# Moving twenty row-scaling products from ScalarE and VectorE to GpSimd, in front of the scatters that read them

## The chip, the cores and the metric

The kernel runs on one core of a Trainium2 chip. The metric is device time of one execution in microseconds (us), the median of several runs. Engines are named as in the profile: PE is TensorE's matmul (PEld its weight load), DVE is VectorE, ACT is ScalarE, POOL is GpSimd, SP is SyncE, which here only issues transfers. Every engine works through its own queue in order, and waits at an instruction whose input is not there yet.

## The reference

Three layers follow each other. The first is a delta-rule attention over 4 batches, 8 heads, 768 positions and head size 48: a 48x48 state per head is read by the query and then updated with each key and value. The second routes each of the 3072 rows of 384 numbers to one of 8 experts. The third is a dense layer with an ELU.

```python
logits = xn @ en.T / tau
expert_idx = np.argmax(logits, axis=1)
probs = np.exp(logits - logits.max(-1, keepdims=True))
probs /= probs.sum(-1, keepdims=True) + 1e-09
gate_w = probs[np.arange(N), expert_idx]
for e in range(E):
    mask = expert_idx == e
    h = np.maximum(x[mask] @ w1[e], 0.0)
    out[mask] = gate_w[mask, None] * (h @ w2[e])
```

The gate weight is positive, so the kernel multiplies each row by it before the expert: `gate * (relu(x w1) w2)` is `relu((gate * x) w1) w2`.

## The kernel before, in words

Attention is done in 12 chunks of 64 positions. A chunk has a chain of solve steps on PE (`chain`, in two halves of the heads), each step evacuated by ACT or DVE; it needs the chunk's prepared keys (`lane`), its queries and values (`rest`), the state that the chunk before left, and the inverse of small triangular blocks. `invert(g)` makes that inverse for the two chunks 2g and 2g+1 at once: on POOL, 30 short tensor-tensor steps that each need the one before (line 1369), then two transposes on DVE (line 1374, `a<-T`), then four transfers into `bdT` (line 1378). The first solve of chunk 2g is the PE group `pw<-rh,bdT` that reads it. Beside these steps POOL prepares keys, queries and values (lines 1107, 1338, 1326), copies blocks for PE (`bd`, line 1220, tiles `bdS`, `bdZ`), and zeroes the next inverse's buffer (lines 1358 and 1360).

A chunk's output leaves PE as rows: `to_rows` puts them into one of four slots of the tile `xt` (line 1529 on ACT or DVE, "xput"). `route` then runs after chunks 1, 3, 5, 7 and 9 on all four slots, and after chunks 10 and 11 on two slots each. It finds each row's expert and place, and its gate weight `gs` (lines 341 and 342 on DVE). Then, for each slot, it multiplies the 384 columns of 128 rows by the gate weight, in place (the "gate" product), and scatters the rows to a buffer in device memory: a one-element memset on POOL (line 347) and an indirect transfer issued by POOL (line 348). After the four scatters POOL adds 128 to the row numbers in `xt` (line 359). A slot can be filled by the next xput only when the scatter that reads it has landed. The routings are numbered 1 to 7 here, in order of time; 1 to 5 have four gate products each.

The gate product has two ways, ACT (line 354) and DVE (line 355). Which way each of the 24 takes stands in the string `WAYS["gate"]`, one digit per product. The order of all work in this stage is fixed by hand: `STARTS` has one number per operation (hundredths of a planned us), and `replay` emits the operations in the order of these numbers. An operation that changes its engine keeps its number, and so its place in that order. The five routings' first gate products have the numbers 14342, 18682, 23603, 27537 and 31581. In the second and the fourth routing two inversion steps follow behind that number and ahead of the first scatter (18688 and 18740, 27546 and 27598), in the first and the third routing one (14389, 23646), in the fifth none. The scatters keep their order: in routing 1, for instance, slots 2, 3, 1, 0.

After attention the experts and the dense layer follow, bound by PE; their first step needs the table of rows that the last routing makes.

Of the kernel before, what the change touches and what calls it, by code (L numbers as in the profile page):

```python
# [12 lines left out]
ALU = mybir.AluOpType  # L13
AX = mybir.AxisListType

NT, DM, NE, F1, F2 = 3072, 384, 8, 1024, 2048
# [190 lines left out]
class Moe(Ops):  # L207
# [92 lines left out]
    def route(self, a, xt, first, step, last):  # L300

        nc, dv, part = self.nc, self.nc.vector, slice(first, None, step)
# [5 lines left out]
        lg, ex, oh, ss, sr, rn, mx, gs, di = (x[:, part] for x in (self.lg, self.ex, self.oh, self.ss, self.sr, self.rn, self.mx, self.gs, self.di))  # L308
# [29 lines left out]
        for b in tiles:  # L338
            a.act(NE + 140, lambda b=b: nc.scalar.activation(out=self.lgp[:, b, 0], in_=self.lg[:, b], func=AF.Exp, scale=self.rn[:, b:b + 1], accum_out=self.gs[:, b:b + 1]),
                  r=["rn", "lg", f"lgp{b}"], w=[f"gs{b}"])  # L340
# [5 lines left out]
        def scatter(b):  # L346
            nc.gpsimd.memset(self.gap, 0.0)
            i = nc.gpsimd.indirect_dma_start(
                out=self.xs, out_offset=bass.IndirectOffsetOnAxis(ap=self.di[:, b:b + 1], axis=0), in_=xt[:, b], in_offset=None)
            apart(self.tc, i, sent)  # L350

        for b in tiles:
            x, g = xt[:, b, :DM], self.gs[:, b:b + 1]
            a.op("gate", ("ACT", DM + 155, lambda x=x, g=g: nc.scalar.activation(out=x, in_=x, func=AF.Copy, scale=g)),
                    ("DVE", DM - 130, lambda x=x, g=g: dv.tensor_scalar(out=x, in0=x, scalar1=g, scalar2=None, op0=ALU.mult)), r=["gs"], w=[f"xt{b}"])
            a.pl.add("POOL", 1.04, lambda b=b: scatter(b), r=[f"xt{b}", "di", f"xid{b}", "xz", *xs], move=0.55)
        if not last:
            xi = xt.bitcast(I32)[:, part, DM]
# [671 lines left out]
class Attn(Ops):  # L1030
# [510 lines left out]
    "clear": "1111201310302011123201",  # L1541
    "dg": "010100100110000111110001001000001010001000100000",
    "evac": "000010001100001010000000000000000001010100000111010000001001000000101000100101000001100000001100000011110001000000010000000001000000011101001010010110000010110001011110011110100000000000001000",
    "gate": "000010010111011011011000",
    "gramA": "675664710346200673657401",
    "gramL": "310001010002161015667366",
    "invert": "111111",
# [208 lines left out]
```

## Time and profile before

| | us |
|---|---|
| median of 3 runs | 953.64 |
| the runs | 951.24, 953.64, 955.93 |
| the profiled execution | 954.83 |
| its span in the profile | 953.4 |

The profiled execution is 1.2 us above the median. A row of the time line of an engine has the start, the duration, the engine, the line of the kernel, the operation, the tiles that it writes and reads, the shape and the count; in brackets at its end stands how long the engine was idle before it and what ended that. Times are us from the start of the span. Attention and routing fill the first 357 us of it.

### The profile page before, as it was taken

The page shows a single profiled execution, that of the slowest core. Times are in us where ns is not written, and L with a number is a line of the kernel's source. Part 1 is how long each engine was busy: PE and PEld are TensorE (multiplying, and loading weights), DVE is VectorE, ACT ScalarE, POOL GpSimd, SP SyncE. Part 2 cuts the span into 40 slices and gives each one's busy share as a digit, 9 for nine tenths or more (in the row PEclk, how much of TensorE's full clock was granted, in tenths as well). Part 3 has the DMA queues.
Part 4 walks back from the last instruction along what each step waited for, and adds up shares of the span by engine and source line. Part 5 has one row for each costly group of instructions (what it writes and reads, how often), then busy time and mean ns, then how long its engine had stood idle before and what let it go on. Part 6 is the DMA issues. An engine that isn't in the chain of part 4 may idle for free.

```text
span 953.4 us, 28791 instructions
## 1 busy us (share of the span) xinstructions
PE 834.9 (88%) x11734; PEld 695.9 (73%) x11735; DVE 768.4 (81%) x1563; ACT 600.4 (63%) x1094; POOL 464.6 (49%) x707
## 2 busy tenths in 40 slices
PE   0537888798999877999999999889999999999995
PEld 0426788687888764555556568789999999999995
DVE  6787878778787963988898988998887887787884
ACT  8896779877786954455646636666545455465652
POOL 6564677676776432143433412354345555355452
PEclk9958999999999997999999999999999999999998
DMA  6667865847545418867899263210010100100000
GB/s 207 163 133 204 235 151 114 177 110 136 131 106 140 148 51 267 174 226 196 238 251 212 92 119 98 84 51 18 1 51 18 51 19 18 35 18 18 18 18 18
DMA packets 115365, 107.58 MB, mean 113 GB/s; under 512 B 72889, under 2 KB 100317, under 8 KB 114973
## 3 DMA queue, kind: packets, MB, share of 16 engines
q1 hardware_dynamic: 108649, 82.98, 35.8%
q0 software_dynamic: 6080, 22.05, 7.5%
q8 instruction: 93, 1.52, 0.7%
q10 hardware_dynamic: 500, 0.68, 0.3%
q14 instruction: 43, 0.35, 0.1%
HBM read 74.72 MB, written 19.97 MB: 99 GB/s over the span
## 4 chain that ended last, share of the span: by engine, by line
PE 49%; DVE 7%; issue 2%; DMA 2%; ACT 1%; SPq 0%; POOL 0%; POOLq 0%; DVEq 0%; ACTq 0%
PE pa L662 17%; PE acc L682 15%; PE acc L620 8%; PE pa L601 8%; DMA st<-in_w 2%; DVE w L519 1%; DVE wbl L676 1%; DVE w L518 1%; DVE dal L534 1%; DVE hl L615 0%; DVE wal L668 0%; SPq L471 0%; DVE dbl L534 0%; DVE wah L669 0%; PE pa L573 0%
## 5 line engine op out<-in xcount | busy, mean ns | idle before, releaser
L682 PE MATMUL acc<-dbh,wbl 128*128 128x192 f16 x672 | 165.3, 246 | 1.4 <-DVE wbl L676 1.4
L682 PE MATMUL acc<-dbl,wbh 128*128 128x192 f16 x672 | 165.3, 246 | 0.9 <-DVE dbl L534 0.9
L682 PE MATMUL acc<-dbh,wbh 128*128 128x192 f16 x672 | 165.3, 246 | 0.2 <-DVE y L630 0.2
L662 PE MATMUL pa<-x,dah 128*128 128x256 f16 x1152 | 157.3, 273 | 1.8 <-DVE wal L668 1.4
L682 PEld LDWEIGHTS <-wbh 128*128 128x128 f16 x1344 | 121.9, 98 | 1.5 <-issue 0.3
L662 PEld LDWEIGHTS <-dah 128*128 128x128 f16 x1152 | 111.9, 98 | 14.7 <-issue 2.0
L662 PE MATMUL pa<-x,dal 128*128 128x256 f16 x576 | 94.4, 273 | 0.9 <-DVE dal L534 0.9
L601 PE MATMUL pa<-x,wah 128*128 128x440 f16 (+6 forms) x384 | 77.0, 337 | 1.9 <-DVE hl L615 1.8
L1223 PEld LDWEIGHTS <-bdKT 112*128 112x128 f16 x1680 | 58.3, 101 | 21.0 <-ACT bdKT L1219 6.1
L1223 PEld LDWEIGHTS <-bdK 128*128 128x128 f16 x960 | 40.8, 119 | 42.8 <-ACT rh L1100 18.5
L669 POOL TENSOR_TENSOR wal<-wal 128x256 f32<-128x256 f32 (+1 forms) x67 | 44.8, 669 | 54.9 <-DVE wal L668 31.1
L675 ACT CAST wbh<-wal 128x384 f16<-128x384 f32 (+1 forms) x73 | 41.3, 566 | 44.8 <-PE acc L682 20.4
L682 PEld LDWEIGHTS <-wbl 128*128 128x128 f16 x672 | 65.7, 98 | 3.1 <-DVE wbl L676 2.1
L620 PE MATMUL acc<-hh,wbh 128*128 128x440 f16 (+6 forms) x192 | 64.2, 334 | 2.0 <-DVE y L630 1.1
L620 PE MATMUL acc<-hl,wbh 128*128 128x440 f16 (+6 forms) x192 | 64.1, 334 | 1.2 <-DVE hl L615 1.1
L614 ACT ACTIVATE hh<-pa 128x440 f16<-128x440 f32 (+6 forms) x64 | 31.9, 504 | 52.2 <-PE acc L620 24.8
L620 PE MATMUL acc<-hh,wbl 128*128 128x440 f16 (+6 forms) x192 | 64.0, 334 | 0.0
L675 ACT CAST wbh<-wah 128x384 f16<-128x384 f32 (+1 forms) x82 | 46.0, 562 | 25.8 <-DVE wah L668 11.3
L1223 PEld LDWEIGHTS <-bdL 128*128 128x128 f16 x1536 | 52.0, 97 | 13.7 <-issue 7.1
L662 PEld LDWEIGHTS <-dal 128*128 128x128 f16 x576 | 56.4, 98 | 7.7 <-DVE dal L534 1.2
L665 ACT ACTIVATE wah<-pa 128x512 f32<-128x512 f32 x48 | 28.6, 596 | 48.4 <-PE pa L662 28.0
L601 PEld LDWEIGHTS <-wah 128*128 128x128 f16 x384 | 37.3, 98 | 29.8 <-issue 3.6
(317 smaller groups left out, 2390.5 us busy)
## 6 DMA issues: line engine op xcount, KB each, us to landing
st<-in_w SPq DMA_DIRECT2D x24, 512.0 KB
st<-in_w SPq DMA_DIRECT2D x32, 384.0 KB
kraw<-in_k SPq DMA_DIRECT2D x22, 384.0 KB
w<-in_w_in POOLq DMA_DIRECT2D x12, 512.0 KB, 6.3
w<-in_w_out POOLq DMA_DIRECT2D x16, 384.0 KB, 5.9
xs_scratch<-in_zeros SPq DMA_DIRECT2D x8, 675.5 KB
raw<-in_q SPq DMA_DIRECT2D x12, 448.0 KB
vraw<-in_v SPq DMA_DIRECT2D x12, 384.0 KB
```

The lines of the kernel that those rows point to most:

```text
L518: self.dve(n, lambda m=m, hi=hi: v.scalar_tensor_tensor(out=m, in0=hi, scalar=-0x40000000, in1=m, op0=ALU.bitwise_and, op1=ALU.bitwise_or) ...
L519: self.dve(n, lambda m=m, lo=lo: v.scalar_tensor_tensor(out=m, in0=lo, scalar=29, in1=m, op0=ALU.logical_shift_right, op1=ALU.bitwise_or), ...
L534: self.dve(n, lambda f=f, part=part: v.scalar_tensor_tensor(out=part("l"), in0=f, scalar=sc, in1=part("h"), op0=ALU.mult, op1=ALU.subtract ...
L601: self.nc.tensor.matmul(self.pa[i][:, :n], lhsT=W[w][:, k, c], rhs=x[:, k, y, t0:t0 + n], start=j == 0 and k == 0, stop=j == 2 and k == 2)
L614: self.act(cap, lambda i, hh=hh: nc.scalar.activation(out=hh, in_=self.pa[i][:, :cap], func=AF.Relu), w=[hn], buf=buf)
L620: nc.tensor.matmul(self.acc[d][:, :cap], lhsT=w[:, f, c], rhs=h, start=f == 0 and j == 0, stop=f == 7 and j == 2)
L662: nc.tensor.matmul(o, lhsT=D[w][:, k, c], rhs=x[:, k, y, t0:t0 + 256], start=q + n + k == 0, stop=n + k == 4, skip_group_check=True)
L665: self.act(512, lambda i, t=t: nc.scalar.activation(out=t, in_=self.pa[i], func=AF.Relu, scale=-1.0 / hs), w=[tn], after=wa, buf=buf)
L669: add = lambda o, x, y, op: [(e, n, lambda w=w: w.tensor_tensor(out=o, in0=x, in1=y, op=op)) for e, n, w in (("POOL", o.shape[1] * 128, nc ...
L675: self.op("ghi", ("ACT", n, lambda f=f, fh=fh: nc.scalar.copy(fh, f)), ("DVE", n / 2, lambda f=f, fh=fh: v.tensor_copy(fh, f)), r=[gn + z] ...
L682: nc.tensor.matmul(self.acc[k][:, o:o + HD], lhsT=h[:, u - 1], rhs=D[d][:, p, w - 1], start=p == 0 and n == 0 and o == FIRST[k], stop=p == ...
L1223: self.nc.tensor.matmul(o, lhsT=l, rhs=r, start=st, stop=True, skip_group_check=True)
```

## The change

The gate product gets a third way, on POOL, and the first twenty products take it. Their numbers in `STARTS` stay, so each stands on POOL's queue where its number puts it among POOL's other work, ahead of the scatter that reads its rows. The last four products (routings 6 and 7) keep the engines that they had.

```diff
             a.op("gate", ("ACT", DM + 155, lambda x=x, g=g: nc.scalar.activation(out=x, in_=x, func=AF.Copy, scale=g)),
-                    ("DVE", DM - 130, lambda x=x, g=g: dv.tensor_scalar(out=x, in0=x, scalar1=g, scalar2=None, op0=ALU.mult)), r=["gs"], w=[f"xt{b}"])
+                    ("DVE", DM - 130, lambda x=x, g=g: dv.tensor_scalar(out=x, in0=x, scalar1=g, scalar2=None, op0=ALU.mult)),
+                    ("POOL", DM, lambda x=x, g=g: nc.gpsimd.tensor_scalar(out=x, in0=x, scalar1=g, scalar2=None, op0=ALU.mult)), r=["gs"], w=[f"xt{b}"])
...
-    "gate": "000010010111011011011000",
+    "gate": "222222222222222222221000",
```

## Rows read from the trace of the kernel before

**Rows 1.** The page, busy time, share of the span and instructions of each engine.

```profile
PE 834.9 (88%) x11734; PEld 695.9 (73%) x11735; DVE 768.4 (81%) x1563; ACT 600.4 (63%) x1094; POOL 464.6 (49%) x707
```

**Rows 2.** Busy time by stretch; the sum is over 150 to 340 us.

```profile
150.00:195.00 45.00, 37.09 (x929) 32.68 (x926) 36.78 (x83) 40.66 (x89) 31.68 (x63) 1.00 0.64 133
...
sum 190.00, PE 168.68 PEld 152.65 DVE 155.84 ACT 151.61 POOL 126.03; mean PE 33.74 PEld 30.53 DVE 31.17 ACT 30.32 POOL 25.21
```

**Rows 3.** The chain that ended last: its first piece (start, duration, what).

```profile
363.68 0.02 SPq L541
```

**Rows 4.** Time line of PE, the first solve of chunks 6 and 10.

```profile
220.31 0.36 PE L1223 MATMUL pw<-rh,bdT 128*128 128x48 f16 x8 [0.41 <-DMA bdT<-a]
...
306.05 0.36 PE L1223 MATMUL pw<-rh,bdT 128*128 128x48 f16 x8 [0.39 <-issue]
```

**Rows 5.** The tile view of `xt` (minimum/median/maximum in ns, first and last start).

```profile
L348 POOL DMA_INDIRECT xs_scratch<-xt,di x24: 958/995/2013, 152.3 to 355.8; - x24
...
L354 ACT ACTIVATE xt<-xt,gs x13: 598/612/618, 151.4 to 353.9; 128x384 f32<-128x384 f32 x13
L355 DVE TENSOR_SCALAR xt<-xt,gs x11: 401/410/481, 194.9 to 349.2; 128x384 f32<-128x384 f32 x11
...
DMA to landing us min/median/max: 2.7/3.2/5.8
```

**Rows 6.** The views of lines 514 and 1326, POOL's rows.

```profile
L514 POOL TENSOR_SCALAR w<-w x3: 1162/1608/1844, 406.2 to 516.0; 128x384 f32<-128x384 f32 x2, 128x512 f32<-128x512 f32 x1
...
L1326 POOL TENSOR_TENSOR vraw<-vraw,n x14: 818/829/1139, 31.8 to 307.4; 128x384 f32<-128x384 f32 x14
```

**Rows 7.** Time line of POOL, the first scatter of routings 1 to 5.

```profile
152.32 1.18 POOL L348 DMA_INDIRECT xs_scratch<-xt,di  x1 [0.98 <-ACT xt L354]
...
195.22 1.05 POOL L348 DMA_INDIRECT xs_scratch<-xt,di  x1 [0.68 <-ACT xt L354]
...
249.52 1.06 POOL L348 DMA_INDIRECT xs_scratch<-xt,di  x1 [0.43 <-ACT z L1100]
...
288.81 1.06 POOL L348 DMA_INDIRECT xs_scratch<-xt,di  x1 [1.62 <-ACT xt L354]
...
328.70 1.17 POOL L348 DMA_INDIRECT xs_scratch<-xt,di  x1 [0.45 <-ACT yT L1508]
```

**Rows 8.** Time line behind routing 1: slot 0's scatter, an inversion step, the xput.

```profile
156.58 0.97 POOL L348 DMA_INDIRECT xs_scratch<-xt,di  x1 [0.22 <-issue]
...
161.03 0.54 DVE L1529 COPY xt<-pw 128x384 f32<-128x384 f32 x1
...
162.74 1.35 POOL L1369 TENSOR_TENSOR T<-T,tmp 128x56 f16<-128x56 f16 x1
```

**Rows 9.** Time line of POOL behind routing 2, ahead of the last inversion step.

```profile
210.08 1.84 POOL L1107 TENSOR_TENSOR Kc<-kraw,Kc 128x384 f16<-128x384 f32 x2 [3.48 <-DVE Kc L1289]
```

**Rows 10.** Time line behind routing 3: the last inversion step, then DVE.

```profile
256.23 0.43 POOL L1369 TENSOR_TENSOR T<-T,tmp 128x30 f16<-128x30 f16 x1
...
257.06 1.29 DVE L1374 STREAM_TRANSPOSE a<-T 128x512 f16<-128x512 f16 x2
...
259.39 0.19 DVE L1531 COPY lgp<-pw 128x32 f32<-128x32 f32 x1 [0.53 <-ACT xt L1529]
...
260.68 0.56 DVE L1432 SCALAR_TENSOR_TENSOR rh<-R,z 128x384 f16<-128x384 f32 x1 [0.63 <-PE R L1223]
```

**Rows 11.** Time line behind routing 4: POOL's value product, ACT behind it.

```profile
294.48 1.60 POOL L1326 TENSOR_TENSOR vraw<-vraw,n 128x384 f32<-128x384 f32 x2
...
296.75 0.48 ACT L1403 COPY R<-vraw 128x384 f32<-128x384 f32 x1 [1.49 <-DVE rh L1432]
297.19 0.49 ACT L1100 ACTIVATE rh<-R 128x384 f16<-128x384 f32 x1
```

**Rows 12.** Time line behind routing 5: POOL's block copy, then PE.

```profile
334.83 1.24 POOL L1220 COPY bdZ<-Zc 64x768 f16<-64x768 f16 x1
...
337.67 0.86 PE L1223 MATMUL pw<-Qc,bdS 112*128 112x64 f16 x24
```

## The prediction, as it was put on record

> **What bounds the kernel now.** I read the page first, then the chain that ended last, then the stretches, then the time lines around the five routings. By the page PE is the busy engine (88%) and POOL is the idlest (49%) [rows 1]; read as an average, that would make POOL the place for more work. The chain that ended last starts only at 363.68 us, with the loads of the expert stage [rows 3]: behind it stands a stage that this change does not touch, and a shift of the attention stage's end moves the whole kernel by about as much. So the question is what sets the pace between 150 and 340 us, where the twenty products stand. There PE is busy 168.68 of 190 us, DVE 155.84, ACT 151.61 and POOL 126.03 [rows 2]: no engine is full, and no engine is idle. PE has 21.3 us of gaps. Busy shares don't say who is late; the waits do. The first solve of chunk 6 waits 0.41 us for the transfer of `bdT`, the inverse that POOL makes, and that of chunk 10 stands behind a gap of 0.39 us that its row puts down to no other engine [rows 4]. So POOL, half idle over the span, has the inverse just in time, and what is put in front of the inversion steps is put in front of PE. That is what the reader is to see: POOL's idle time lies where it waits for inputs, not where it would have to take the products.
>
> **What is removed.** Of the twenty products, ten are on ACT and ten on DVE (the digits of the string), at 0.61 and 0.41 us [rows 5]: 6.1 us leave ACT and 4.1 us leave DVE. And POOL's wait for the first product of each routing goes: 0.98, 0.68, 0.43, 1.62 and 0.45 us [rows 7]; its later scatters wait about 0.2 us each, before and after. Some of the wait comes back in another form, below.
>
> **What is added: the price of one product on POOL.** The trace has no such product by a per-row factor. The nearest row is POOL's tensor-scalar instruction on f32: 1.16 and 1.61 us for 128x384, and 1.84 us for 128x512 [rows 6]. The next is its tensor-tensor product on 128x384 f32, 0.83 us in the middle of 14 (an issue in two halves; each row is one half) [rows 6]; it has one input more and would be the lower end. The upper end is 1.61 us. I take 1.16: same instruction, same shape, and in attention POOL's rows lie near their minimum (0.82 to 0.83 us for half of the 14). Twenty of them add 23.2 us to POOL.
>
> *A page weighed against the row.* The Trainium skill ("GPSIMD Engine Reference", Engine selection) says that one-input elementwise work on GpSimd runs at about line rate. By that and its 1.2 GHz the product would be an estimated 0.32 us and a fixed part, well under the row, and the sum would come out near the second rival. The row of 1.16 us speaks against it, and its row of 1.84 us for 512 columns too.
>
> **How far POOL's queue is pushed back.** Four products are 4.64 us a routing; the wait that they replace is taken off. In routing 4 the wait does not go: the first product stands ahead of two inversion steps that used to run while ACT multiplied, so POOL now waits for `gs` where it ran them, and about the 1.62 us of before is idle again. I count it as not saved. The pushes are then 3.7 (routing 1), 4.0 (2), 4.2 (3), 4.7 (4; 4.64 and a little) and 4.2 us (5). Behind the waiting product stand the inversion steps, the value and query products, the block copies and the scatters with their transfers, whose number stays. No transfer of SP is passed.
>
> **What of a push reaches PE.** Each is followed to the first thing that was just in time.
> - Routing 1: slot 0's scatter starts at 156.58 and its rows land 2.7 us later at the least [rows 8, 5], at 159.3. Pushed by 3.7 that is 163.0. The xput that refills slot 0 stands at 161.03 on DVE [rows 8], so DVE waits 2.0 us, with the transposes for the inverse of chunks 4 and 5 behind it. Reaches: 2.0.
> - Routing 2: POOL idles 3.48 us ahead of the key product at 210.08, behind which the last inversion step stands [rows 9]. 4.0 less 3.48 is 0.5.
> - Routing 3: the last inversion step ends at 256.66 and DVE takes the transposes at 257.06 [rows 10]: 0.4 of cover. DVE then waits 3.8 us; its gaps of 0.53 and 0.63 up to the solve's evacuation at 260.68 [rows 10] take back 1.2. Reaches: 2.6.
> - Routing 4: POOL's value product ends at 296.08, and ACT's copy of it stands at 296.75, with the evacuation `rh<-R` of the running chain right behind it [rows 11]. 4.7 less 0.7 is 4.0 us in which ACT stands still; the inverse of chunks 10 and 11, for which PE already waits, is as late. Reaches: 4.0.
> - Routing 5: the copy of `bdZ` ends at 336.07 and PE reads it at 337.67 [rows 12]: 1.6 of cover, so 2.6 reaches.
>
> Together 11.7 us. What comes back: the 10.2 us taken off ACT and DVE. Nothing comes back at the bound of zero, 5.1 if the two engines' mean set the pace throughout; I take the middle, 2.5, since a product stands right in front of a chain evacuation in only part of the cases. And PE's gaps are 11% of the stretch [rows 2], so of 11.7 us some 1.3 is absorbed. The sum is 11.7 - 2.5 - 1.3 = 7.9 us: 954.83 + 7.9 = 962.7 for the profiled execution, which lies 1.2 above the median of the runs; against the median, 961.6. I say 962.
>
> **Ends of the range.** At 1.61 us a product each push grows by 1.8, all of it past the covers: 11.7 + 9 - 3.8 = 16.9, 970.5 against the median. At 0.83 each shrinks by 1.3: 0.7 + 0 + 1.3 + 2.7 + 1.3 = 6.0, less 3.8 is 2.2: 955.8. With the whole 5.1 given back it is 953.2.
>
> **Rivals.**
> 1. *The products are dearer, because POOL and DVE get in each other's way.* For: an inversion step of 128x56 took 1.35 us [rows 8], while one of 128x30, half as wide, took 0.43 [rows 10]; one product of 128x384 took 1.61. Against: the median of the 0.83 us rows is close to their minimum. Time: up to 970. The Trainium skill ("SBUF — State Buffer", Who interferes with whom) states a port pair that GpSimd shares with VectorE and that one instruction at a time holds; the step of 1.35 us agrees with it, and by that rule the price would lie nearer to 1.61.
> 2. *The products cost POOL little, or POOL's push is taken up.* At 0.61 us, ACT's price, a push is 2.2 smaller: routings 1, 2 and 5 hide (1.5, 1.8 and 2.0 against covers of 1.7, 3.48 and 1.6, so 0.4), 3 and 4 give 0.4 and 1.8; 2.6 less 2.5 is nothing: 953.6, no change. The page named above would have it so. Against: no f32 row of POOL with 384 columns is under 0.8 us.
> 3. *Faster: ACT and DVE set the pace.* ACT is busy 40.66 of 45 us in the first stretch [rows 2]. If the pushes hide and half of the 10.2 us reaches the end, it is 5.1 less: 948.5. It decides where a product costs POOL no more than 0.6 us. Against: chunks 6 and 10 wait for POOL's product, not for ACT [rows 4].
> That the products don't go to POOL can't be: the string says so.
>
> **How the numbers follow.** What a measurement of this kernel can tell from no change is about 0.5%, 4.8 us: slower begins at 958.4, faster at 948.9. Forecast (a price of 1.0 to 1.4 us, pushes reach PE): 0.52. Rival 1: 0.14, slower. Rival 2, with the cases of 0.83 us and of a push that is taken up: 0.25, no change. Rival 3: 0.09. Slower 0.66, same 0.25, faster 0.09. The range from 953 to 970 leaves out rival 3, part of the no-change cases (those below 953), and the tail above: about 2 in 10.
>
> **What the changed profile would show.** Line 356 or so, a POOL tensor-scalar on `xt`, twenty times at about 1.16 us; ACT and DVE with ten fewer each; no wait of a first scatter on ACT. POOL's inverse (the step of 128x30 that ends each) later against the routing by 3 to 5 us; ACT idle some 5 us, not 1.49, ahead of the copy of routing 4's stretch, with POOL as its releaser; DVE idle ahead of the transposes after routing 3 and of the xput after routing 1; the first experts' load later by what the time grows. The prediction is wrong if a product costs 0.6 us or less, or if these waits are there and the chain that starts at 363.68 does not move: then the gaps of PE took up more than 1.3 us.

## The result, and the profile after

The kernel changed takes 967.92 us (median of 5 runs, 966.42 to 969.98) where the kernel before took 953.52 beside it: a ratio of 1.0142, 95% interval [1.0114, 1.0169], so 13.5 us slower (10.9 to 16.1). The forecast was 962, range 953 to 970. In the changed kernel, lines from 356 on stand one further down than in the rows of before.

The page's busy line and the stretches, which answer to [rows 1, 2]:

```profile
PE 839.9 (87%) x11734; PEld 699.5 (72%) x11735; DVE 768.6 (80%) x1553; ACT 596.0 (62%) x1084; POOL 488.0 (50%) x727
```

```profile
150.00:195.00 45.00, 35.15 (x828) 30.79 (x828) 33.34 (x72) 34.69 (x75) 33.93 (x59) 0.96 0.66 136
...
sum 190.00, PE 160.79 PEld 144.42 DVE 145.63 ACT 139.53 POOL 138.99; mean PE 40.20 PEld 36.10 DVE 36.41 ACT 34.88 POOL 34.75
```

POOL has 20 instructions and 23.4 us more, DVE and ACT ten instructions fewer each. In the 190 us from 150 on PE is busy 7.9 us less than before, DVE 10.2 and ACT 12.1 less, POOL 13 more. Of the 10.2 and 12.1 the moved products themselves are 4.1 and 6.1. What is left, some 6 to 8 us on each of the three engines, is the same work standing later: they wait more.

The tile view of `xt` in the changed kernel, from 140 to 370 us, which answers to [rows 5]:

```profile
L356 POOL TENSOR_SCALAR xt<-xt,gs x20: 1238/1261/1627, 152.4 to 346.9; 128x384 f32<-128x384 f32 x20
...
DMA to landing us min/median/max: 2.7/3.6/4.9
```

A product costs 1.26 us in the middle; the forecast took 1.16. The waits of the changed kernel behind routings 1 (150 to 172 us), 3 (252 to 275), 4 (293 to 312) and 5 (338 to 356); columns: who waited for whom, us in all, times, longest:

```profile
DVE xt L1530 <- DMA xs_scratch<-xt,di: 4.6, 1, 4.6
...
PE pw L1224 <- DVE bdS L1220: 2.7, 1, 2.7
```

```profile
DVE a L1375 <- POOL T L1370: 3.2, 1, 3.2
...
PE pw L1224 <- DVE rh L1433: 1.8, 2, 1.3
```

```profile
DVE a L1375 <- POOL T L1370: 5.7, 1, 5.7
ACT R L1404 <- POOL vraw L1327: 5.6, 1, 5.6
...
PE pw L1224 <- ACT rh L1101: 3.5, 1, 3.5
...
POOL xt L356 <- DVE gs L342: 1.1, 1, 1.1
```

```profile
ACT xt L1530 <- DMA xs_scratch<-xt,di: 2.5, 1, 2.5
...
PE pw L1224 <- POOL bdZ L1221: 1.2, 1, 1.2
```

These are the waits that the forecast named: the xput for the scatter's landing, the transposes for the last inversion step, ACT's copy for the value product, PE for the copy of `bdZ`. PE's own wait at routing 1 is one that it did not name: for the copy of `bdS` that DVE makes behind the xput. Routing 4 in the time lines of POOL and then of ACT, which answer to [rows 11]:

```profile
295.62 1.25 POOL L356 TENSOR_SCALAR xt<-xt,gs 128x384 f32<-128x384 f32 x1 [1.07 <-DVE gs L342]
...
298.99 4.04 POOL L356 TENSOR_SCALAR xt<-xt,gs 128x384 f32<-128x384 f32 x3
...
307.46 1.61 POOL L1327 TENSOR_TENSOR vraw<-vraw,n 128x384 f32<-128x384 f32 x2
```

```profile
308.32 0.48 ACT L1404 COPY R<-vraw 128x384 f32<-128x384 f32 x1 [5.65 <-POOL vraw L1327]
308.73 0.48 ACT L1101 ACTIVATE rh<-R 128x384 f16<-128x384 f32 x1
```

ACT stands 5.65 us ahead of its copy where it stood 1.49 [rows 11], and the evacuation right behind it is what PE then waits 3.5 us for.

To see where the time comes in, each PE instruction of the attention stage is set against the same one (the same place in PE's program) of the kernel before. The table gives by how much it starts later, at six places named by their time in the kernel before; the places are chosen so that one routing's effect lies between two neighbours. The profiled execution of the kernel before was taken twice (span 953.4 both times) and the changed kernel twice (966.5 and 970.4), so there are two pairs. The two traces of the kernel before differ by up to 3.2 us between two places of this table, in transfers' landing times above all; a step in it is certain to some 2 us.

```
us later than the kernel before      150.5  205.3  251.6  290.2  330.3  344.6
changed, first pair                    1.1    4.0    4.7    7.6   13.3   14.7
changed, second pair                   4.6    5.0    6.8   10.2   15.8   17.2
step between (mean of the pairs)              1.7    1.2    3.2    5.6    1.4
routing in that step                            1      2      3      4      5
```

From 150.5 us on 13.1 us come in (13.6 and 12.6; paired crosswise, the four traces give 15.8 and 10.4), and nearly all of it reaches the end. In the first pair PE is 14.7 us late at 344.6, SP issues the first experts' load at 378.01 us, 14.2 later than before (363.82, behind the chain's first piece of [rows 3]), and the span is 13.1 longer.

### The profile page after: what moved, and what is told of

Its sections match the earlier page's. It is cut to its first block, busy times and chain, and to the rows that moved or that the text cites. A ratio compares the mean times of both kernels' runs of the same rounds, so it can differ in the third digit from the quotient of the medians.

```text
span 966.5 us, 28797 instructions
## 1 busy us (share of the span) xinstructions
PE 839.9 (87%) x11734; PEld 699.5 (72%) x11735; DVE 768.6 (80%) x1553; ACT 596.0 (62%) x1084; POOL 488.0 (50%) x727
## 4 chain that ended last, share of the span: by engine, by line
PE 55%; DVE 9%; POOL 4%; issue 3%; DMA 3%; ACT 2%; ACTq 0%; SPq 0%; POOLq 0%; DVEq 0%
PE pa L663 17%; PE acc L683 15%; PE pa L602 9%; PE acc L621 9%; PE pw L1224 3%; POOL xt L356 2%; POOL xs_scratch L348 1%; PE R L1224 1%; DVE w L520 1%; DMA bdKT<-KTc 1%; DVE wbl L677 1%; PE pw L1520 1%; DVE w L519 1%; DMA bdS<-Sc 1%; DVE dal L535 1%
## 5 line engine op out<-in xcount | busy, mean ns | idle before, releaser
L676 ACT CAST wbh<-wah 128x384 f16<-128x384 f32 (+1 forms) x82 | 46.0, 562 | 25.5 <-DVE wah L669 11.3
```

Source lines behind the costliest of these rows:

```text
L676: self.op("ghi", ("ACT", n, lambda f=f, fh=fh: nc.scalar.copy(fh, f)), ("DVE", n / 2, lambda f=f, fh=fh: v.tensor_copy(fh, f)), r=[gn + z] ...
```

## The experiments

Ratios are to the kernel before, run beside it on the same chip; us are that ratio times the median of before, with the 95% interval. The runs fell on three chips. On two of them the kernel before takes 954.43 and 955.10 us; on the third it takes 975.35. That difference is a finding of its own, below. Each run's chip is named with it; that of the result above is not on record, and the kernel before took 953.52 there.

**One routing alone.** The string gives POOL the four products of one routing, and leaves the others where they were. For routing 1:

```diff
-    "gate": "222222222222222222221000",
+    "gate": "222210010111011011011000",
```

Expected of routings 1 to 5:

> Only routing 1's four products go to POOL; the other sixteen stay on ACT and DVE. Theory (each routing has its own first wait, so each costs its own amount): the xput that refills slot 0 waits for the late scatter, and the transposes behind it; I forecast 2.0 us for this place, and the changed kernel showed a wait of 4.6 us there, so now I expect +2 to +4 us: 955.5 to 957.5. Rival (each product costs the same wherever it stands, a fifth of the whole loss for each routing): +2.7 us. Rival (the loss is not at this routing): 0.

> Only routing 2's four products go to POOL. Theory: POOL idles 3.48 us ahead of the key product behind them, so the push is nearly taken up: I forecast 0.5 us reaching PE before anything is given back, so 0 to +0.5 us: 953.5 to 954. Rival (each product costs the same wherever it stands): +2.7 us, 956.2.

> Only routing 3's four products go to POOL. Theory: the last inversion step comes about 3.8 us late, and DVE waits with the transposes: 2.6 us reach the solve, less what is given back, so +1.5 to +3 us: 955 to 956.5. Rival (each product costs the same): +2.7 us, which this run alone can't tell from the theory; what tells them apart is its difference to routings 2 and 4.

> Only routing 4's four products go to POOL, in front of two inversion steps and of the value product that ACT copies. Theory: it is the dearest of the five, 4.0 us by the forecast, up to 5.5 by the shift of PE in the changed kernel: 957.5 to 959. Rival (each product costs the same): +2.7 us, 956.2.

> Only routing 5's four products go to POOL. Theory: the block copy that PE reads has 1.6 us of cover against a push of 4.2, so 2.6 us at most and +1 to +2.6 us: 954.5 to 956. Rival (each product costs the same wherever it stands): +2.7 us, 956.2.

Measured:

| products on POOL | ratio, 95% | us more than before | chip near |
|---|---|---|---|
| routing 1 | 1.0058 [1.0029, 1.0087] | 5.5 (2.8 to 8.3) | 955 |
| routing 2 | 1.0036 [1.0007, 1.0065] | 3.4 (0.7 to 6.2) | 955 |
| routing 3 | 1.0057 [1.0026, 1.0088] | 5.4 (2.5 to 8.4) | 955 |
| routing 4 | 1.0053 [1.0025, 1.0082] | 5.1 (2.4 to 7.8) | 955 |
| routing 5 | 0.9958 [0.9935, 0.9982] | -4.1 (-6.3 to -1.8) | 975 |

The times do not settle what they were made for. Each of routings 1 to 4 is slower by itself, but the intervals are nearly 6 us wide. Three of the four hold the rival's 2.7 us for every routing, the fourth begins at 2.8, and one price of some 5 us for each would fit all four. Routing 2 cost more than the 0 to 0.5 us of the theory: a miss. Together the four give 19.4 us, more than the 13.5 of the whole change; with four such intervals it is not shown that the parts don't add up. What the traces show is sharper, though they were taken in some of the fastest executions of these kernels (955.83 us with routing 1 alone and 954.46 with routing 3, where the medians are 960.08 and 959.70). In the run with routing 4 alone, the waits from 280 to 306 us:

```profile
DVE a L1375 <- POOL T L1370: 5.9, 1, 5.9
ACT R L1404 <- POOL vraw L1327: 5.8, 1, 5.8
...
PE pw L1224 <- ACT rh L1101: 3.7, 1, 3.7
```

That is routing 4 of the whole change to within 0.2 us, with three untouched routings ahead of it: its waits are its own. With routing 3 alone, from 240 to 270 us, and with routing 1 alone, from 145 to 170 us:

```profile
DVE a L1375 <- POOL T L1370: 4.4, 1, 4.4
```

```profile
DVE xt L1530 <- DMA xs_scratch<-xt,di: 4.4, 1, 4.4
```

PE's step at the routing that was changed is 1.5 us for routing 1, 2.1 for 2, 4.7 for 3 and 4.4 for 4 against the second trace of before, and 2.7, 1.9, 4.9 and 6.4 against the first. Routings 3 and 4 are the dear ones, as in the table above; the order within each pair lies inside its 2 us. With routing 5 alone its step is 1.9 us against either trace; but on that chip the kernel without products has 1.1 and 0.4 there too, so what routing 5 costs by itself is not settled. With routing 2 alone, 3.1 us more (5.1 against the first trace) come in at routing 4's place, where nothing had been changed; what set them there is open.

**What comes back from ACT and DVE.** The first twenty products are made by no engine (the rows go to the experts without their gate weight, so this leaves out part of the computation). POOL gets nothing in their place.

```diff
-                    ("POOL", DM, lambda x=x, g=g: nc.gpsimd.tensor_scalar(out=x, in0=x, scalar1=g, scalar2=None, op0=ALU.mult)), r=["gs"], w=[f"xt{b}"])
+                    ("NONE", 0, lambda: None), r=["gs"], w=[f"xt{b}"])
```

> The first twenty products are left out of every engine (this leaves out part of the computation), so that the 10.2 us come off ACT and DVE and nothing is added to POOL, whose wait for the first product goes too. It measures the term that I gave as 2.5 us with bounds of 0 and 5.1. By the forecast the time is 951, by the upper bound 948.5, by the lower 953.5. The shift of PE in the changed kernel adds up to nearly the whole loss without any give-back, so I now lean to 0 to 2.5.

> The first twenty products left out of every engine (this leaves out part of the computation), a second time. In the first set its ratio to before was 1.0049 where before took 975: the 10.2 us taken off ACT and DVE gave nothing back there. Where before is near 954: 951 by my forecast of 2.5 us, 948.5 by the upper bound, 953.5 if nothing comes back. Where before is near 975: again 1.005.

The first of the two ran on the chip near 975: 1.0049 [1.0025, 1.0073] to its before, 4.8 us slower with less work. The second ran on a chip near 955: 954.82 us, 0.9996 [0.9972, 1.002], so -0.4 us (-2.7 to 1.9). Ten us off ACT and DVE are worth nothing that shows. The measurement is nearest to the lower bound of the forecast's term (0); the 2.5 that it took lies just inside the interval's end, rival 3's 5.1 well outside.

**The push alone.** All products stay on ACT and DVE; POOL makes one of the same kind at the same twenty places, on a tile `pad` that nobody reads, with 304 columns for want of room.

```diff
+        self.pad = t("pad", [128, 304])
...
+            idle = lambda g=g: last or nc.gpsimd.tensor_scalar(out=self.pad, in0=self.pad, scalar1=g, scalar2=None, op0=ALU.mult)
+            a.op("gate", ("ACT", DM + 155, lambda x=x, g=g, idle=idle: (idle(), nc.scalar.activation(out=x, in_=x, func=AF.Copy, scale=g))),
+                    ("DVE", DM - 130, lambda x=x, g=g, idle=idle: (idle(), dv.tensor_scalar(out=x, in0=x, scalar1=g, scalar2=None, op0=ALU.mult))), r=["gs"], w=[f"xt{b}"])
...
+    "gate": "000010010111011011011000",
```

> All products stay on ACT and DVE as in the kernel before; POOL makes at the same twenty places a product of the same kind on a scratch tile that nobody reads, 304 columns wide in place of 384 (about 1.0 us each by the 1.26 of 384 columns, an estimate). It measures the push alone, without relief for ACT and DVE. Theory: the push is the whole cause, so the kernel is as slow as the changed one or slower, less a fifth for the shorter products: 962 to 969. Rival (part of the loss comes from the real products' data, which POOL and the scatters of the same rows need in turn): the time stays under 960.

The tile view of `pad`:

```profile
L355 POOL TENSOR_SCALAR pad<-pad,gs x20: 1042/1056/1867, 148.4 to 341.6; 128x304 f32<-128x304 f32 x20
```

965.39 us, within the 962 to 969 that the theory gave; but it ran on the chip near 975, where that is 0.9894 [0.9861, 0.9927] of the kernel before, 10.3 us faster. As a test of the push against the kernel before, its time is spoilt by that chip. Its trace still shows waits of the changed kernel where no product left ACT or DVE: 2.9 us of DVE's transposes for the last inversion step at routing 3, 2.5 us of ACT's copy for the value product at routing 4, 1.5 us of PE for the copy of `bdZ` at routing 5. What its time stands beside is taken up with the stops, below.

**Slot 0 first.** The changed kernel with slot 0's product and scatter ahead of the other three in routings 1, 2 and 5; in routing 1 the order is 0, 2, 3, 1. Only the numbers of these operations in `STARTS` change.

```diff
+MOVED = {646: 14342, 647: 14430, 650: 14404, 651: 14563, 652: 14466, 653: 14696, 648: 14576, 649: 14829,
...
+STARTS = tuple(MOVED.get(i, x) for i, x in enumerate(STARTS))
```

> The changed kernel, with slot 0's product and scatter put first of the four in routings 1, 2 and 5 (last in 1 and 2, third in 5); POOL's work and its end are the same. Theory: in the changed kernel the xput that refills slot 0 waits 4.6, 2.8 and 2.5 us for that scatter's landing in these routings; with it first that wait goes, and what is left of routing 1 is the late inverse behind it. So 2 to 6 us come back: 962 to 966 against 967.9. Rival (the late inverse alone sets PE, and the xput's wait is beside it): no change, 967 to 969.

970.48 us on the chip near 975, 0.9959 [0.9942, 0.9976] of before there; the changed kernel took 967.92 and 971.77 elsewhere. DVE's xput and transposes behind routing 1, in its time line:

```profile
160.65 0.55 DVE L1530 COPY xt<-pw 128x384 f32<-128x384 f32 x1
...
168.36 1.31 DVE L1375 STREAM_TRANSPOSE a<-T 128x512 f16<-128x512 f16 x2
```

and the same xput in the changed kernel:

```profile
167.21 0.56 DVE L1530 COPY xt<-pw 128x384 f32<-128x384 f32 x1 [4.56 <-DMA xs_scratch<-xt,di]
```

The wait of 4.56 us is gone, and so is that of routing 2 (2.8 us in the changed kernel, none here). PE's step at routing 1, from 150.5 to 205.3 us, isn't: 4.1 us against the first trace of before, 2.9 against the second, where the changed kernel has 2.9 and 0.4. Taken by itself that would speak for the rival. But the step comes in at another place. The table gives by how much PE falls behind the first trace of before in two parts of that step (the second trace gives the same picture within 1 us):

```
us that come in                            150.5 to 162   162 to 172   chip near
changed kernel, its two traces              0.4, -0.2       2.9, 2.5       955
routing 1 alone                                  -0.3            3.3       955
without products                                 -0.3            0.0       955
slot 0 first                                      3.3           -0.1       975
push alone                                        2.8           -0.4       975
routing 5 alone (routing 1 as before)             4.7           -0.1       975
without products                                  4.5            0.0       975
```

The second part is where DVE, behind the xput, makes the copy of `bdS` for which PE waits in the changed kernel, and not with slot 0 first:

```profile
168.68 1.46 PE L1224 MATMUL pw<-Qc,bdS 112*128 112x64 f16 x24 [2.65 <-DVE bdS L1220]
```

```profile
163.96 0.86 PE L1224 MATMUL pw<-Qc,bdS 112*128 112x64 f16 x24
```

So slot 0 first takes away the 2.5 to 2.9 us that the xput's wait brings in, and PE waits there for no inverse either. The 3.3 us that stand in their place come in beside the scatters, in every run on that chip, whether routing 1 was changed or not. The theory of this run holds in routing 1; what the order is worth in time on a chip near 955 was not measured.

**The kernels again, on one chip, and a version with the scatters apart.** Four kernels on a chip near 955: the kernel before for a trace, the changed one, the one without products (above), and the kernel before with its scatters put between steps that POOL does anyway:

```diff
+MOVED = {651: 14430, 799: 14563, 800: 14605, 647: 14646, 801: 14779, 802: 14819, 653: 14859,
...
+STARTS = tuple(MOVED.get(i, x) for i, x in enumerate(STARTS))
```

> The kernel before itself, for a trace of the same chip as the next three. In the second set of runs the kernel before took 975.35 us where it took 954.43 in the first, and the trace of the run with only routing 5's products on POOL showed PE, ACT and DVE without work for 2 to 5 us in each of the first four routings, beside scatters that no product of POOL stood between. If that is a state of the chip, this trace shows such stops where the time is near 975, and none where it is near 954.

> The changed kernel itself. Theory (late scatters and inverses): slower than before by the same 13 us on any chip, a ratio of 1.014. Rival (on a chip where PE, ACT and DVE stop beside back-to-back scatters, the products of POOL between them take the stops away): the ratio is under 1 where before is near 975, some 966 to 970 us, and 1.014 only where before is near 954.

> The kernel before, with all products on ACT and DVE, and the four scatters of each of the first five routings put between steps that POOL does anyway (two inversion steps after each scatter in routings 1 and 4, one in 2 and 3, the copy of bdZ ahead of the last in 5); slot 0's scatter second in routing 1. POOL's work and the end of its inverse stay as they are. If the distance between scatters is what the stops depend on: 5 to 15 us faster than before where before is near 975, and no change (within 3 us) where it is near 954. If the stops have another cause: no change in either case.

The kernel before: 954.83 us. The changed kernel: 971.77, 1.017 [1.0143, 1.0198], 16.2 us more (13.7 to 18.9); the loss is there a second time. The version with the scatters apart: 959.49, 1.004 [1.0017, 1.0064], 3.8 us more where no change was expected. It gains nothing on this chip, and it was not run on the one near 975, where it might have gained. No version that ran beats the kernel before on the chips near 955.

## Why the prediction was right, and where its sum was off

**What bounds the kernel.** Right. POOL was idle half the span before and is idle half of it after, and at each routing another engine waits for something that stands behind its products. The chain that ended last now runs through the products themselves: from 140 to 372 us its view by line puts 6.5% on `POOL xt L356` and 5.4% on the scatters' line 348, behind PE's 11.4%, where the chain of before began behind them [rows 3]. The forecast's opening puts the inverse in front of PE; in the changed kernel it is mostly something else. PE's waits at routings 1, 3, 4 and 5 are for DVE's copy of `bdS`, an evacuation on DVE behind the transposes, one on ACT, and POOL's copy of `bdZ`. For the inverse's transfer its weight load waits once, 1.7 us behind routing 1 in one trace and 0.4 in the other. Nor did chunk 10 wait for the inverse before, as the prediction's routing 4 and its third rival say: its row names no engine [rows 4].

**The price.** 1.26 us for 1.16, inside the range taken; the twenty take 26.4 us together (1.325 in the mean), 3.2 more than the 23.2 forecast. Rival 2 falls with it: it needed 0.61. What the Trainium skill ("GPSIMD Engine Reference", Engine selection) says of one-input work, about line rate, on which that rival leaned, differs from the measurement, and the measurement decides: 1.26 us for 384 columns and 1.06 for 304, against the 0.83 that POOL's two-input rows took for 384 [rows 6]. Rival 1 (dearer products) has a little in it: five of the twenty took 1.43 to 1.63 us, and with routing 3 alone the four took 1.26, 1.56 and 1.69 us at minimum, median and maximum. The median of all twenty, near the minimum of 1.24, says that it is no rule. The Trainium skill ("SBUF — State Buffer", Who interferes with whom) has GpSimd share a port pair with VectorE; whether that is behind the dear ones no run here shows.

**What of the push reaches PE.** Predicted 2.0, 0.5, 2.6, 4.0 and 2.6 us for routings 1 to 5, together 11.7; in the traces 1.7, 1.2, 3.2, 5.6 and 1.4, together 13.1. Routing 4 is the dearest in both, with its copy on ACT as the place, and no routing is off by more than the 2 us to which a step is certain. Within that, these were read wrongly:

- Routing 1: the number holds by some luck, the road to it in part. The xput did wait, 4.6 us and not 2.0, because slot 0's scatter began at 162.64 and was read out only at 167.2, 4.5 later, where the forecast used the least landing time, 2.7 us [rows 5]. What PE waits for behind it is first the copy of `bdS`, 2.7 us (1.8 in the second trace), and only then the transposes' inverse. Some of it is made up again by 205.3 us, where the step ends.
- Routing 2: the key product's wait took up most of the push, as argued; the xput's wait of 2.8 us was not seen coming.
- Routing 4: ACT's idle time ahead of its copy grew by 4.2 us (5.65 for 1.49), near the 4.0 forecast, and PE waited 3.5 us for the evacuation behind it. The step of 5.6 is 1.6 more than forecast, within its 2 us. POOL waited 1.07 us for `gs` where the forecast had 1.62; its four products took 5.3 us for 4.64.
- Routing 5: the row of 337.67 that the forecast took for the reader of `bdZ` reads `bdS` [rows 12]. The reader is the row at 338.57, so the cover was 2.5 us and not 1.6, and by the forecast's own sum 4.2 less 2.5 is 1.7. PE waited 1.2 us for `bdZ`, and the step is 1.4. The reader before and after:

```profile
338.57 0.86 PE L1223 MATMUL pw<-Ac,bdZ 128*128 128x64 f16 x24
```

```profile
353.28 0.88 PE L1224 MATMUL pw<-Ac,bdZ 128*128 128x64 f16 x24 [1.24 <-POOL bdZ L1221]
```

**What comes back.** Here the sum was off: 2.5 us from the relief of ACT and DVE and 1.3 us from PE's gaps, together 3.8. With the products taken off and nothing added, the time moves by -0.4 us (-2.7 to 1.9), nearest to nothing. ACT and DVE were not what the stretch waited for, which the same section of the prediction had read from the waits; the middle of two bounds was taken against that reading. The 1.3 us of the gaps have no run of their own: PE's steps are what is left after its gaps, so they can't show what the gaps took up. With nothing given back the forecast's own sum is 954.83 + 11.7 = 966.5, or 965.3 against the median. An estimate from the rows above adds the 3.2 us of the dearer products and takes off the 0.9 of routing 5's cover: 967.6, beside the 967.92 measured. So the forecast was 6 us low because it counted a give-back that no run shows and counted the products too cheap; the misread cover of routing 5 made up a little of that.

**What stays open.** The changed kernel starts its first routing 1.1 and 4.6 us later than the kernel before. Both of its traces have a wait of PE for the transfer into `bdKT` between 122 and 145 us, 2.8 and 3.0 us long, where the traces of before have 0.5 and 1.2; the version with the scatters apart has 2.5, the one without products has 0.3, but so has the push alone, and slot 0 first has 1.0. No instruction ahead of that place was changed. Nor do the runs say whether the four routings alone really add up to more than the whole.

## What to carry to other kernels

An engine that is idle for half of the span is not spare if its idle time is waiting and its work has to be in time: follow its queue from the place where work is put in to the first thing that another engine takes from it, and count what of the push is left there. Work taken off engines that nobody waits for gave nothing back that a run could measure, so it is no credit in the sum without a wait that shows it. When a row is taken for the reader of a tile, read the tile's name in it. And before a step in a trace is put down to a change, look for the same step in a run on the same chip where that place was left alone.

## What the runs showed of the hardware that was not expected

One chip ran the kernel before in 975.35 us, the other two in 954.43 and 955.10, and it did so in 29 runs (970.32 to 979.13). These runs stand in one set, so whether the chip or its condition at that time is behind it isn't shown. Without products the kernel was slow there too: 978.86 (954.82 elsewhere). But the two kernels that had products of POOL among the scatters of all five routings, slot 0 first and the push alone, took 970.48 and 965.39, near to what the changed kernel takes elsewhere (967.92, 971.77). So the push alone is 10.3 us faster than the kernel before there. Slot 0 first is 4.0 faster, no more than routing 5 alone (972.17, 4.1 faster), which has the products in one routing only.

The traces show where. The windows of the kernel without products on that chip, beside routing 2's scatters (198.0 to 202.9 us); columns: stretch, its length, busy us and instructions of PE, PEld, DVE, ACT and POOL, granted clock, DMA share, GB/s:

```profile
198.00:200.00 2.00, 1.62 (x51) 1.54 (x48) 1.40 (x3) 0.00 (x0) 1.79 (x3) 1.00 0.67 207
200.00:202.00 2.00, 0.92 (x14) 0.56 (x13) 0.00 (x0) 0.59 (x1) 1.55 (x5) 0.95 0.49 187
202.00:204.00 2.00, 0.95 (x12) 0.64 (x13) 0.00 (x0) 0.22 (x1) 1.83 (x4) 0.50 0.53 198
204.00:208.00 4.00, 3.89 (x82) 3.61 (x80) 2.59 (x7) 2.60 (x6) 0.14 (x1) 0.50 0.70 135
```

and the same kernel on a chip near 955, from routing 2's first scatter on:

```profile
195.00:197.00 2.00, 2.00 (x66) 1.98 (x65) 1.82 (x3) 0.70 (x3) 1.84 (x3) 1.00 0.66 194
197.00:199.00 2.00, 2.00 (x78) 2.00 (x75) 1.48 (x4) 2.00 (x5) 1.78 (x3) 1.00 0.62 163
199.00:201.00 2.00, 2.00 (x68) 1.87 (x65) 1.71 (x5) 1.96 (x5) 1.69 (x5) 1.00 0.96 237
```

While POOL issues scatter after scatter, PE comes down to 12 matmuls in 2 us, and DVE starts nothing from 200 to 204 us. PE does not stand at one wait; in its time line there it goes on a few matmuls at a time:

```profile
200.10 0.25 PE L1224 MATMUL pw<-Qc,bdS 112*128 112x64 f16 x3
200.78 0.28 PE L1224 MATMUL pw<-Qc,bdS 112*128 112x64 f16 x4 [0.42 <-issue]
201.50 0.31 PE L1224 MATMUL pw<-Qc,bdS 112*128 112x64 f16 x5 [0.45 <-issue]
202.22 0.39 PE L1224 MATMUL pw<-Qc,bdS 112*128 112x64 f16 x4 [0.41 <-issue]
```

Added up from the traces, PE, ACT and DVE are idle all three at once for 11.3 us between 140 and 345 us of this run, and for 1.4 us in the same kernel on the chip near 955. With routing 5 alone it is 5.7 us in all on the slow chip, not the 2 to 5 us in each of four routings of which the expectation for the second trace of before speaks. With slot 0 first and with the push alone it is 3.2 and 3.4, and the changed kernel has 4.1 and 4.0 where before takes near 955. Even so these two are not free of it: at routing 1 they fall 3.3 and 2.8 us behind beside the scatters (the table under slot 0), where the kernels without products between those scatters fall 4.5 and 4.7 behind. And after such a stop the granted clock is 0.50 (1.2 of 2.4 GHz) for the 4 us and more that follow, so a stop costs again behind it. What holds the instructions up, and whether it is the distance between the scatters or the products themselves that takes the stops away, is not shown: the version with the scatters apart ran on a chip that has no such stops, and neither the kernel before nor the changed one was traced on the chip that has them. That the changed kernel would be the faster of the two there is inferred from its two near relatives, not measured.
